# A SwiGLU kernel's first loads: which engine's queue issues the transposing load of tokens 256 to 511, and in which order the first matmul groups run

## The chip, the cores and the metric

The kernel runs on one core of one Trainium2 chip. The metric is the device time of one execution in microseconds (us). A separate profiled execution gives the page and the trace; its times count from the start of its span.

## What is computed

```
x: (1, 2048, 512), w_gate, w_up: (512, 1376), w_down: (1376, 512), all bf16
g = silu(x @ w_gate)
u = x @ w_up
out = (g * u) @ w_down
```

## The kernel before

TensorE contracts over 128 partitions, so x is needed transposed: `xT_sb` holds x as [128 of D, 4 slices of D, 2048 tokens]. The hidden size 1376 is cut into ten full slices of 128 and a rest of 96. The tokens are worked in four chunks `c` of 512 (`SC`). For each chunk and each full slice `ft` there is a gate group (kind G) and an up group (kind U): four matmuls over D each into one PSUM bank. ScalarE takes silu of the gate's bank into `sg_sb` (L280), VectorE multiplies it with the up bank into `hT_sb` (L289). The rest of 96 is done in groups X (L370) and Y (L381). After all chunks the groups O multiply by w_down (L394, L408, L431), VectorE and ScalarE copy the banks to `o_sb`, and SyncE stores them.

All engines run their instructions in program order, with semaphores between them. The part that the change touches is the start, which works on tokens 0 to 511:

- The first half of chunk 0, tokens 0 to 255 (`HT` = 256), comes by a plain load `xn` (256 KB) and is transposed on TensorE against an identity matrix (groups T, L346). VectorE and ScalarE copy the four results to `xT_sb` (L293, L280), ScalarE those of the upper half of D.
- The second half, tokens 256 to 511, comes by a transposing DMA, `x0b` (`load_x`, L87). So do the later chunks, `x1` to `x3`.
- The gate and up weights come in slabs of slices: `wg0`/`wu0` (slice 0, 128 KB each), `wg1`/`wu1` (slice 1, 128 KB each), `wg2`/`wu2` (two slices), `wg4`/`wu4` (three) and `wg7`/`wu7` (the rest), by `load_w` (L92). `wut` is the last 32 columns of w_up.
- `loads_on_scalar` issues `wg0` and `wu0` from ScalarE's queue; `loads_on_sync` issues all others from SyncE's queue in the order written there. After its issues ScalarE runs a dummy activation (L269), ahead of which stands the load of its function table.
- TensorE starts with eight matmuls on constants (L337: six of 512 columns, two of 128). It then waits for `xn` and runs the transposes.
- Then come the groups of slices 0 and 1, named `g0`, `u0`, `g1`, `u1` in the code. They are run in pieces, since tokens 0 to 255 are there earlier than 256 to 511: `g0` and `u0` on tokens 0 to 127 and 128 to 255 (eight matmuls of 128 columns each), `g1` and `u1` on tokens 0 to 255 (four of 256 columns each), and then all four on tokens 256 to 511 (four of 256 columns each). `gu_matmuls` waits (`need`) for the loads that a piece reads. From slice 2 on a group is four matmuls of 512 columns.

The order of the pieces before:

```
for g in (g0, u0):
    gu_matmuls(g, 0, P)
    gu_matmuls(g, P, HT)
gu_matmuls(g1, 0, HT)
gu_matmuls(u1, 0, HT)
for g in (g0, u0, g1, u1):
    gu_matmuls(g, HT, SC)
```

Of the kernel before, what the change touches and what calls it, by code (L numbers as in the profile page):

```python
# [13 lines left out]
def bass_standalone__swiglu_ffn__prompt_kernel(nc, x, w_gate, w_up, w_down, out):  # L14
# [7 lines left out]
    SC = 512  # L22
# [6 lines left out]
    HT = SC // 2  # L29
# [15 lines left out]
    with ExitStack() as es:  # L45
# [29 lines left out]
        loads = {}  # L75

        def load_sem(name):
            loads[name] = sem(f"s_{name}")
            return loads[name]
# [6 lines left out]
        def load_x(eng, name, t0, t1):  # L86
            eng.dma_start_transpose(  # L87
                xT_sb[:, :, t0:t1], xf[t0:t1, :]
            ).then_inc(load_sem(name), 16)

        def load_w(eng, name, src, base, f0, f1):
            eng.dma_start(  # L92
                w_sb[:, :, base + f0:base + f1],
                src[:, f0:f1].rearrange("(k p) f -> p k f", p=P),
            ).then_inc(load_sem(name), 16)

        slabs = [(0, 1), (1, 2), (2, 4), (4, 7), (7, NFT)]
        slab_of = {ft: a for a, b in slabs for ft in range(a, b)}

        def load_slab(eng, a, b):  # L100
            load_w(eng, f"wg{a}", w_gate, 0, a * P, min(b * P, F))
            load_w(eng, f"wu{a}", w_up, UPH, a * P, min(b * P, F - 32))

        def loads_on_scalar(act):
            load_slab(act, *slabs[0])

        def loads_on_sync(sp):
            sp.dma_start(
                xn_sb[:, :, :].rearrange("p j d -> p (j d)"), xf[0:HT, :].rearrange("(p j) d -> p (j d)", j=NXN)
            ).then_inc(load_sem("xn"), 16)  # L110
            load_slab(sp, *slabs[1])
            load_x(sp, "x0b", HT, SC)
            for a, b in slabs[2:]:
                load_slab(sp, a, b)
            load_w(sp, "wut", w_up, F - (F - 32), F - 32, F)
            for c in range(1, NSC):
                load_x(sp, f"x{c}", c * SC, (c + 1) * SC)
            sp.dma_start(
                wd_sb[:, 0:NFF, :], w_down[0:NFF * P, :].rearrange("(k p) d -> p k d", p=P)
            ).then_inc(load_sem("wd"), 16)  # L120
            for c in range(NSC):
                sp.dma_start(
                    wdt_sb[R * c:R * (c + 1), :, :], w_down[NFF * P:F, :].rearrange("(q p) d -> p q d", p=R)
                ).then_inc(load_sem(f"wdt{c}"), 16)
            sp.dma_start(wdl_sb[:, :], w_down[NFF * P:F, LASTA:D]).then_inc(load_sem("wdl"), 16)
# [7 lines left out]
        def add_group(kind, **what):  # L133
            g = dict(kind=kind, at=len(groups), bank=banks[len(groups) % NB], readers=[], **what)
            groups.append(g)
            return g
# [71 lines left out]
        for i in range(NXN):  # L208
            for h, eng in enumerate("DA"):
                g = add_group("T", i=i, h=h)  # L210
                op = add_op(
                    eng, g, kind="copy", out=xT_sb[:, 2 * h:2 * h + 2, i * P:(i + 1) * P],
# [15 lines left out]
        for at in range(NST):  # L228
# [5 lines left out]
            for c0, c1 in halves:  # L234
                g = add_group("O", t=t, c0=c0, c1=c1, c=c)
                if c0 == 0:
                    quads[j].append(g)
                else:
# [3 lines left out]
                    eng, g, kind="copy", out=o_sb[ob][:, c0:c1], src=g["bank"][:, 0:c1 - c0],  # L242
# [6 lines left out]
        def rows_of(t):  # L249
            if t < NXN:  # L250
                return of[0:HT, :].rearrange("(p j) d -> j p d", j=NXN)[t]
            return of[t * P:(t + 1) * P, :]

        def on_sync(sp):
            loads_on_sync(sp)
            for t, c0, c1, ob, eng, n in stores:
                sp.wait_ge(s_A if eng == "A" else s_D, n)
                sp.dma_start(rows_of(t)[:, c0:c1], o_sb[ob][:, c0:c1]).then_inc(s_out[ob], 16)
            for i in range(NOS):
                sp.wait_ge(s_out[i], 16 * n_store[i])  # L260

        def on_gpsimd(pool):
            pool.iota(
                diag[:, :], pattern=[[-1, P]], base=0, channel_multiplier=1,
            ).then_inc(s_I, 1)

        def on_scalar(act):
            loads_on_scalar(act)
            act.activation(adummy[:, 0:4], zero_c, ACT.Silu)  # L269
            for op in act_ops:  # L270
                act.wait_ge(s_P, op["g"]["at"] + 1)
                if op["kind"] == "silu":
                    if op["free"]:
                        act.wait_ge(s_D, op["free"])
                    fn = ACT.Silu
                else:
                    if op["stored"][1]:
                        act.wait_ge(*op["stored"])
                    fn = ACT.Copy
                act.activation(op["out"], op["src"], fn).then_inc(s_A, 1)  # L280
# [15 lines left out]
        def on_tensor(pe):  # L296
            landed = set()

            def need(name):
                if name not in landed:  # L300
                    pe.wait_ge(loads[name], 16)
                    landed.add(name)
# [3 lines left out]
            def after(eng, n):  # L306
                if n > read[eng]:
                    pe.wait_ge(s_A if eng == "A" else s_D, n)
                    read[eng] = n
# [6 lines left out]
            def gu_matmuls(g, n0, n1):  # L316
                c, ft = g["c"], g["ft"]
                if c > 0:
                    need(f"x{c}")
                if c == 0 and n1 > HT:  # L320
                    need("x0b")
                need(("wg" if g["kind"] == "G" else "wu") + str(slab_of[ft]))
                col = (0 if g["kind"] == "G" else UPH) + ft * P
                for dk in range(KD):
                    if c == 0 and dk % 2 == 0:
                        for i in range(n0 // P, min(n1 // P, NXN)):
                            after(*xt_ready[i, dk // 2])
                    ins = pe.matmul(  # L328
                        g["bank"][:, n0:n1], lhsT=w_sb[:, dk, col:col + P],
                        rhs=xT_sb[:, dk, c * SC + n0:c * SC + n1], start=(dk == 0), stop=(dk == KD - 1),  # L330
                    )
                if n1 == SC:
                    ins.then_inc(s_P, 1)
# [15 lines left out]
            g0, u0, g1, u1 = groups[NT:NT + 4]  # L349
            for g in (g0, u0):  # L350
                gu_matmuls(g, 0, P)
                gu_matmuls(g, P, HT)
            gu_matmuls(g1, 0, HT)
            gu_matmuls(u1, 0, HT)
            for g in (g0, u0, g1, u1):
                gu_matmuls(g, HT, SC)

            for g in groups[NT + 4:]:
                kind = g["kind"]
# [73 lines left out]
                skip_group_check=True,  # L433
            ).then_inc(s_P, 1)

        on_sync(nc.sync)
        on_gpsimd(nc.gpsimd)
        on_scalar(nc.scalar)
        on_tensor(nc.tensor)
        on_vector(nc.vector)  # L440

# [27 lines left out]
```

## Time and profile before

| | |
|---|---|
| median of 3 runs | 120.57 us (120.52 to 120.98) |
| the profiled execution's own time | 120.32 us |
| its span | 118.9 us |
| granted TensorE clock, mean over the span | 1.00 |
| TensorE (PE) busy | 115.4 us, 97% |
| VectorE (DVE) busy | 47.3 us, 40% |
| ScalarE (ACT) busy | 31.0 us, 26% |
| DMA queue q1 (SyncE's) | 8.48 MB, 26.7% of 16 engines' span |
| DMA queue q10 (ScalarE's) | 0.26 MB, 1.0% of 16 engines' span |

The span goes from the first to the last of the program's own instructions; the time of the execution has some more around it. PEld is TensorE's weight load, which runs beside its matmuls. A name with a q behind it (SPq, ACTq) is an engine's sequencer, which issues DMAs. In the views a duration of one instruction is in ns and all else in us. "Idle before" is what an engine waited ahead of a group of instructions, and the name behind the arrow is what ended most of that wait. The time "to landing" of a DMA runs from the start of its issue to the semaphore that tells of its last byte. In the timeline the first two columns are start and duration. Some records of matmuls are missing from the trace.

### The profile page before, as it was taken

To read this page: it belongs to the slowest core of one execution; us is meant where nothing else is said; L and a number is where in the kernel's file an instruction comes from. 1 tells how busy PE (TensorE), PEld (TensorE's weight loads), DVE (VectorE), ACT (ScalarE), POOL (GpSimd) and SP (SyncE) were. 2 spreads that over 40 slices of the span, in tenths; PEclk is the share of its full clock that TensorE was granted. 3 is DMA by queue.
4 is the path that set the end of the run, shared out by engine and by line. 5 is a ranking of instruction groups with operands and counts; after the bars stand their busy time and mean duration, and the time that the engine had idled before them with its cause. 6 is when DMAs were issued, how large, how long until landed. Compare 5 with 4: busy or idle time off the path is not lost.

```text
span 118.9 us, 1519 instructions
## 1 busy us (share of the span) xinstructions
PE 115.4 (97%) x600; PEld 54.1 (45%) x611; DVE 47.3 (40%) x73; ACT 31.0 (26%) x53; POOL 0.4 (0%) x5
## 2 busy tenths in 40 slices
PE   7999999999999999999999999999999999999993
PEld 2774444444444444444444444344434444444452
DVE  0133443353443444433444334469617422006530
ACT  4344324454234363244262343230000000000001
POOL 1000000000000000000000000000000000000000
PEclk9999999999999999999999999999999999999999
DMA  3999999970000000000000000000004221002412
GB/s 103 271 307 357 264 162 242 328 183 24 0 0 0 6 0 0 0 3 3 0 0 0 6 0 0 0 0 0 0 0 138 88 88 44 0 0 75 145 50 88
DMA packets 17559, 8.84 MB, mean 74 GB/s; under 512 B 10640, under 2 KB 17424, under 8 KB 17552
## 3 DMA queue, kind: packets, MB, share of 16 engines
q1 hardware_dynamic: 16496, 8.48, 26.7%
q10 hardware_dynamic: 1056, 0.26, 1.0%
q8 instruction: 5, 0.08, 0.3%
q14 instruction: 2, 0.02, 0.1%
HBM read 4.81 MB, written 2.10 MB: 58 GB/s over the span
## 4 chain that ended last, share of the span: by engine, by line
PE 97%; issue 1%; DVE 0%
PE bank L328 58%; PE bank L394 29%; PE bank L370 3%; PE bank L337 2%; PE bank L408 2%; PE bank L381 2%; PE bank L346 1%; DVE o_sb L293 0%; PE bank L431 0%
## 5 line engine op out<-in xcount | busy, mean ns | idle before, releaser
L328 PE MATMUL bank<-xT_sb,w_sb 128*128 128x512 bf16 (+2 forms) x338 | 69.7, 364 | 0.4
L328 PEld LDWEIGHTS bank<-xT_sb,w_sb 128*128 128x128 bf16 x344 | 32.8, 98 | 36.4 <-issue 0.2
L289 DVE TENSOR_TENSOR hT_sb<-sg_sb,bank 128x512 bf16<-128x512 f32 x40 | 27.5, 688 | 40.5 <-PE bank L328 36.6
L394 PE MATMUL bank<-wd_sb,hT_sb 128*128 128x512 bf16 (+2 forms) x166 | 34.5, 366 | 0.4 <-issue 0.3
L280 ACT ACTIVATE sg_sb<-bank 128x512 f32<-128x512 f32 x40 | 23.8, 596 | 40.8 <-PE bank L328 40.8
L394 PEld LDWEIGHTS bank<-wd_sb,hT_sb 128*128 128x128 bf16 x170 | 16.1, 98 | 19.1 <-issue 1.3
L293 DVE CAST o_sb<-bank 128x512 bf16<-128x512 f32 (+1 forms) x16 | 10.1, 663 | 22.0 <-PE bank L408 12.3
L280 ACT ACTIVATE o_sb<-bank 128x384 bf16<-128x384 f32 x1 | 0.5, 492 | 37.8 <-PE bank L394 37.8
L289 DVE TENSOR_TENSOR ht_sb<-sgy_sb,bank 32x512 bf16<-32x512 f32 x8 | 5.5, 684 | 0.2
L289 DVE TENSOR_TENSOR ht_sb<-sgx_sb,bank 32x512 bf16<-32x512 f32 x4 | 2.8, 691 | 3.5 <-ACT sgx_sb L280 3.5
L370 PE MATMUL bank<-xT_sb,w_sb 128*128 128x512 bf16 x15 | 4.1, 379 | 0.1
L337 PE MATMUL bank<-const-bfloat16-1.0 128*128 128x512 bf16 (+1 forms) x8 | 2.9, 545 | 0.8 <-PEq L454 0.8
L280 ACT ACTIVATE sgx_sb<-bank 32x512 f32<-32x512 f32 x4 | 2.4, 588 | 4.5 <-PE bank L370 4.5
L408 PE MATMUL bank<-wdt_sb,ht_sb 32*128 32x512 bf16 (+1 forms) x48 | 2.9, 372 | 0.0
L370 PEld LDWEIGHTS bank<-xT_sb,w_sb 128*128 128x128 bf16 x16 | 1.6, 98 | 1.9
L280 ACT ACTIVATE sgy_sb<-bank 64x512 f32<-64x512 f32 x4 | 2.4, 590 | 0.1
L337 PEld LDWEIGHTS bank<-const-bfloat16-1.0 128*128 128x128 bf16 x8 | 1.0, 136 | 2.4 <-issue 2.4
L381 PE MATMUL bank<-xT_sb,w_sb 128*64 128x512 bf16 x16 | 1.9, 382 | 0.0
L408 PEld LDWEIGHTS bank<-wdt_sb,ht_sb 32*128 32x128 bf16 x48 | 1.1, 93 | 1.7 <-issue 0.8
L269 ACT ACT_TABLE_LOAD x1 | 1.3, 1283 | 1.8 <-issue 1.8
L293 DVE COPY xT_sb<-bank 128x256 bf16<-128x256 bf16 x2 | 0.6, 292 | 2.7 <-PE bank L346 2.7
L381 PEld LDWEIGHTS bank<-xT_sb,w_sb 128*64 128x64 bf16 x16 | 0.8, 109 | 1.0 <-DVE hT_sb L289 0.4
(14 smaller groups left out, 4.0 us busy)
## 6 DMA issues: line engine op xcount, KB each, us to landing
out_dram<-o_sb SPq DMA_DIRECT2D x15, 128.0 KB, 1.7
wd_sb<-in_w_down_dram SPq DMA_DIRECT2D x1, 1280.0 KB, 9.2
w_sb<-in_w_gate_dram SPq DMA_DIRECT2D x1, 480.0 KB, 5.9
w_sb<-in_w_up_dram SPq DMA_DIRECT2D x1, 448.0 KB, 6.5
w_sb<-in_w_gate_dram SPq DMA_DIRECT2D x1, 384.0 KB, 4.5
w_sb<-in_w_up_dram SPq DMA_DIRECT2D x1, 384.0 KB, 5.1
wdt_sb<-in_w_down_dram SPq DMA_DIRECT2D x4, 96.0 KB, 7.5
xn_sb<-in_x_dram SPq DMA_DIRECT2D x1, 256.0 KB, 2.8
```

What stands on the lines that cost most here:

```text
L269: act.activation(adummy[:, 0:4], zero_c, ACT.Silu)
L280: act.activation(op["out"], op["src"], fn).then_inc(s_A, 1)
L289: ins = dve.tensor_tensor(op["out"], op["a"], op["b"], ALU.mult)
L293: ins = dve.tensor_copy(op["out"], op["src"])
L328: ins = pe.matmul(g["bank"][:, n0:n1], lhsT=w_sb[:, dk, col:col + P], rhs=xT_sb[:, dk, c * SC + n0:c * SC + n1], start=(dk == 0), stop=(dk ...
L337: pe.matmul(banks[NB - 1][:, 0:width], lhsT=ones_w, rhs=ones_m[:, 0:width], start=True, stop=True)
L346: ins = pe.transpose(tview(g["bank"])[:, k, :], xn_sb[:, g["i"], dk * P:(dk + 1) * P], ident[:, :])
L370: ins = pe.matmul(g["bank"][:, :], lhsT=w_sb[:, dk, XC0:XC0 + P], rhs=xT_sb[:, dk, c * SC:(c + 1) * SC], start=(dk == 0), stop=(dk == KD - 1),
L381: ins = pe.matmul(g["bank"][y0:y1, :], lhsT=w_sb[:, dk, YC0:YC0 + 64], rhs=xT_sb[:, dk, c * SC:(c + 1) * SC], start=(dk == 0), stop=(dk == ...
L394: ins = pe.matmul(g["bank"][:, 0:c1 - c0], lhsT=hT_sb[:, fk, t * P:(t + 1) * P], rhs=wd_sb[:, fk, c0:c1], start=(start and fk == 0), stop= ...
L408: ins = pe.matmul(g["bank"][:, 0:c1 - c0], lhsT=ht_sb[R * c:R * (c + 1), q, j * P:(j + 1) * P], rhs=wdt_sb[R * c:R * (c + 1), q, c0:c1], s ...
```

## The change

ScalarE issues one DMA ahead of its table load instead of two: the transposing load `x0b`. SyncE issues `xn` and then all slabs in order, `wg0` and `wu0` among them, and `x0b` no longer. Ahead of the next transposing load, `x1`, SyncE waits for the landing of `x0b`. On TensorE the pieces of `g0`, `u0` and `g1` on tokens 256 to 511 run ahead of the two pieces of `u1`. The engines' programs are also written down in another order (ScalarE's first), so that the semaphore of `x0b` exists when SyncE's program names it; each engine's own order isn't touched by that.

```diff
         def loads_on_scalar(act):
-            load_slab(act, *slabs[0])
+            load_x(act, "x0b", HT, SC)
 
         def loads_on_sync(sp):
             sp.dma_start(
                 xn_sb[:, :, :].rearrange("p j d -> p (j d)"), xf[0:HT, :].rearrange("(p j) d -> p (j d)", j=NXN)
             ).then_inc(load_sem("xn"), 16)
+            load_slab(sp, *slabs[0])
             load_slab(sp, *slabs[1])
-            load_x(sp, "x0b", HT, SC)
             for a, b in slabs[2:]:
                 load_slab(sp, a, b)
             load_w(sp, "wut", w_up, F - (F - 32), F - 32, F)
+            sp.wait_ge(loads["x0b"], 16)
             for c in range(1, NSC):
                 load_x(sp, f"x{c}", c * SC, (c + 1) * SC)
...
             gu_matmuls(g1, 0, HT)
+            for g in (g0, u0, g1):
+                gu_matmuls(g, HT, SC)
             gu_matmuls(u1, 0, HT)
-            for g in (g0, u0, g1, u1):
-                gu_matmuls(g, HT, SC)
+            gu_matmuls(u1, HT, SC)
...
+        on_scalar(nc.scalar)
         on_sync(nc.sync)
         on_gpsimd(nc.gpsimd)
-        on_scalar(nc.scalar)
         on_tensor(nc.tensor)
         on_vector(nc.vector)
```

## The prediction

> **What bounds the kernel now.** I read the page's busy times and chain first, then the chain in order of time, then the timeline of the first 9 us by engine, the tile view of the activations, and last the DMA view of the first 4 us.
>
> ```profile
> PE 115.4 (97%) x600; PEld 54.1 (45%) x611; DVE 47.3 (40%) x73; ACT 31.0 (26%) x53; POOL 0.4 (0%) x5
> ```
>
> TensorE is busy 115.4 of 118.9 us, so nothing that only moves other engines can gain. The chain in order of time shows what is left of its idleness at the front:
>
> ```profile
> 0.77 2.93 PE bank L337 x8
> 3.71 0.70 PE bank L346 x8
> 4.41 0.07 issue
> 4.47 3.87 PE bank L328 x40
> 8.35 0.05 issue
> 8.40 10.74 PE bank L328 x49
> ```
>
> Warm-up, eight transposes, then matmuls without a break. The pieces "issue 0.05" come about every 49 matmuls; 600 matmul records stand against 611 weight loads, so a piece of that kind is a lost record, not a stall. The change touches only what lies before 8.4 us. Who waits there:
>
> ```profile
> PEld bank L328 <- issue: 0.2, 1, 0.2
> PEld bank L328 <- DMA xT_sb<-in_x_dram: 0.2, 1, 0.2
> PEld bank L346 <- issue: 0.2, 1, 0.2
> ```
>
> The middle line is the one wait for the load that the change hurries, x0b. In the single records x0b lands at 6.38, the next weight load starts at 6.42 and its matmul at 6.42 instead of 6.37: the matmuls lost 0.05 us. That is all an earlier x0b can win. The wait at L346 is for xn: it lands at 3.49, the transposes start at 3.63, the first copies at 4.04 and 4.22, the first matmul at 4.47. Any delay of xn goes through this path.
>
> The timeline of ScalarE and SyncE, then the four transposing loads in the tile view (duration min/median/max in ns):
>
> ```profile
> 0.73 0.46 ACTq L92 DMA_DIRECT2D w_sb<-in_w_gate_dram  x1
> 1.22 0.53 ACTq L92 DMA_DIRECT2D w_sb<-in_w_up_dram  x1
> 1.78 1.28 ACT L269 ACT_TABLE_LOAD   x1 [1.78 <-issue]
> 4.22 0.66 ACT L280 ACTIVATE xT_sb<-bank 128x256 bf16<-128x256 bf16 x2 [0.94 <-PE bank L346]
> ...
> L87 SPq DMA_TRANSPOSE xT_sb<-in_x_dram x4: 1690/2386/4537, 2.2 to 16.5; - x4
> ```
>
> ScalarE's order is issue, table load, dummy, transpose copies, and it has 0.94 us to spare before the copies. The DMA view of 0 to 4 us, one slice per 0.1 us:
>
> ```profile
> GB/s 0 0 0 0 0 0 0 0 0 0 0 0 0 0 0 0 0 41 225 246 328 287 328 307 351 136 126 220 225 287 266 233 189 210 243 279 279 292 287 287
> ...
> xn_sb<-in_x_dram SPq DMA_DIRECT2D x1, 256.0 KB, 2.8
> w_sb<-in_w_gate_dram ACTq DMA_DIRECT2D x1, 128.0 KB, 3.2
> w_sb<-in_w_gate_dram SPq DMA_DIRECT2D x1, 128.0 KB, 3.4
> w_sb<-in_w_up_dram ACTq DMA_DIRECT2D x1, 128.0 KB, 3.7
> w_sb<-in_w_up_dram SPq DMA_DIRECT2D x1, 128.0 KB, 3.7
> xT_sb<-in_x_dram SPq DMA_TRANSPOSE x1, 4.2
> ```
>
> Two facts. First, the engines move data from 1.7 us on and are full, some 285 GB/s with 256-byte packets, from 3.5 us, so the order of bytes decides. Second, xn ran alone at about 300 GB/s until 2.45; then ScalarE's first packets came, the total fell to 126, and xn's last 25 of 128 packets (51 KB) took 0.55 us, 93 GB/s by the packet records, while ScalarE's queue moved 50 KB. Whatever shares xn's time slows xn.
>
> **The change part by part.** *Issues.* ScalarE loses two issues (0.46 + 0.53) and gains one DMA_TRANSPOSE. The trace has none on ScalarE and none on an empty queue. Bounds: a plain issue, 0.46, and the longest of the four, 4.54. I take 1.7, the row with the same 256 tokens; 1.8 was measured for one with twice the tokens, and the longer ones end just as earlier loads on SyncE's queue drain. Then 0.73 + 1.7 = 2.43, table load 1.28, dummy 0.20: ScalarE is ready at 3.95, before 4.22: cost nothing, with 0.27 us of cover. Beyond an issue of 1.97 each further us is paid in full.
>
> *Weights.* SyncE's second and third loads now are wg0 and wu0, of the size and shape of wg1 and wu1, which stood there. ScalarE's queue carried 1,024 packets of 256 bytes (page: 1,056 with completions, 0.26 MB) and carries 1,024 such packets again, those of x0b. So the nearest rows for wg0 and wu0 are the landings of wg1 and wu1: 1.20 + 3.4 = 4.58 and 1.66 + 3.7 = 5.33. wg1 and wu1 follow at 128 KB each by 282 GB/s, 0.46 us: 5.79 and 6.25. The lower bound, had the DMA been full since 1.7 us, is some 0.35 us earlier for each, and then none is late.
>
> *Order on TensorE.* No matmul is added. Twelve 256-column matmuls (12 x 0.109 = 1.31 us) move ahead of u1, so wu1's due time goes from 5.94 to 7.25 and x0b's from 6.37 to 5.94. x0b's place on ScalarE's queue is that of wg0 and wu0, landed by 4.87; with the transpose's slower issue I take 5 to 5.5. Both are covered.
>
> *SyncE's wait.* Behind it are x1 to x3 and all of w_down. SyncE gets there at about 8 us (ten weight issues of 0.41 to 0.58 and one of 1.44 from 1.2 on), after x0b's landing even in the before trace (6.38): no stall. Were it 3 us, x1, landed 16.97 and first used at about 23.0, would still be in time. Cost 0, cover 6 us.
>
> *The sum, weights alone.* wg0 at 4.58 plus the 0.07 from landing to matmul: g0 starts 4.65 instead of 4.47; eight matmuls of 0.056 end at 5.10; wu0 lets u0 start at 5.37, end 5.82; wg1 lets g1 start at 5.84 instead of 5.50, end 6.28; 1.31 us of second halves end at 7.59; u1, eight times 0.109, at 8.46. Before it was 8.18. So **+0.28 us**; by the lower bound of the landings -0.05 us.
>
> *The sum, xn.* What share xn loses depends on when x0b's first packet comes, which no row shows. Earliest: 0.73 + 0.87 (the stores' issue to first packet) = 1.60; latest: 2.45, when wg0's came. By the count of packets x2's first came 1.35 us after its issue, behind those of x1, so I take 2.05. Of xn 94 packets, 192 KB, are then left: 51 KB in the first 0.55 us, as in the row, and 141 KB at half of 285 GB/s, 0.99 us; xn ends at 3.59 instead of 3.02, +0.57. The latest start gives 0; the earliest, before any of xn, +0.8 (256 KB from 1.7: 0.55 + 205 / 142 = 2.0, an end at 3.7 to 3.8). A late xn also lets the transposes run after 4.02, where the spacing of the 128-column matmuls falls from 0.107 to 0.056, which gives back 0.1; x0b's 0.05 is gained. So xn alone gives +0.42 (bounds -0.05 and +0.65), and it hides the late wg0, wu0 and wg1 (first due at 4.47 + 0.47, landed 4.58). The two sums are not added: they are the same bytes met at different gates. I take **+0.4 us**.
>
> [...]
>
> The profiled execution took 120.32, its span 118.9 plus 1.4 around it: 120.72 after. It lies 0.25 below the median of the three runs, 120.57, so on their scale I forecast 121.0.
>
> **The rivals.**
>
> *ScalarE comes late (slower).* If its transposing issue takes as long as the third such row, 2.98, it ends at 3.71, the table load and dummy at 5.2, and the copies start 1.0 us after 4.22. The first accumulation needs ScalarE's half, so the loss is about +1.0 less 0.05: 121.5. It decides from an issue of 1.97 us. For: only 0.27 us of cover, and ScalarE's plain issues are some 10% slower than SyncE's (0.46 to 0.41). Against: the long rows had a loaded queue ahead; this one is first. 12%.
>
> *xn held behind all of x0b (slower).* ScalarE's issue starts 8 ns before SyncE's. If the 1,024 packets go first, xn's data waits 1.0 us (x0b's own packets took 4.8 to 5.75), xn lands at 4.4 and the loss is some +0.85: 121.4. For: nothing but the order of issue. Against: wg0 was issued 8 ns earlier too and came 0.7 us after xn. 11%.
>
> *TensorE's clock rises late (slower).* The warm-up matmuls are spaced 0.427 us at 512 columns, later ones 0.216; the step is at 4.02. The warm-up ends at 3.5, exactly when xn lands. [...] The granted clock in the profile's rows is 1.00 throughout and does not show the step, so no row prices a hole. 5%. [...]
>
> *x0b's packets come late (slightly faster).* If they start after 3.0, xn is alone to its end, lands near 3.1, the transposes follow the warm-up at 3.53, wg0 and wu0 land in time and x0b still lands before 5.94: -0.15, so 120.4. For: a transposing issue may hand out packets slowly. Against: x2's 1.35 us. 12%.
>
> **How the numbers follow.** 0.5% of 120.57 is 0.6 us, about what a measurement of this kernel can tell from no change. The likeliest case (60%) is 121.0, its own range 120.5 to 121.3, its upper end past 0.6. No path gives a gain of 0.6, since the idle time that can be removed is 0.05 to 0.2: faster 0.02. Slower by 0.6 or more: 12 + 11 + 5, and some 6 from the likeliest case: 0.34. Same: 0.64. The range runs from the fast rival, 120.4, to 121.8, above the first two slow rivals' prices; it leaves out the clock's rival and the tails.
>
> **What would show it.** In the changed profile: xn's landing (3.49 before) moves to 3.7 to 4.2; TensorE's first L328 matmul to 4.65 to 5.0; wg0 and wu0 land near 4.6 and 5.3; the wait for x0b is gone; the stretch from 8.5 us on has the old length. ScalarE's DMA_TRANSPOSE below 1.97 us and its copies released by TensorE, not by the table load, would rule out the first rival. The forecast is wrong if the first 512-column matmul (8.18 before) starts later than 8.8 or earlier than 8.0, or if a wait appears after it.

## The result, and the profile after

| | before | after |
|---|---|---|
| median of 13 runs each | 120.76 us (120.31 to 121.31) | 121.12 us (120.88 to 123.2) |
| ratio after / before | | 1.0041, 95% interval 1.0025 to 1.0057 |
| the profiled execution, its span | 120.32, 118.9 us | 121.26, 119.9 us |

Ratios leave out executions more than 1.5% above the fastest of their kernel (of the changed kernel the one at 123.2). By the ratio the change costs 0.3 to 0.7 us, 0.5 in the middle: slower, with the middle (0.41%) below the 0.5% that the chances were drawn by and the upper end (0.57%) above it. The forecast was +0.4 us.

The two profiled executions differ by 1.0 us of span, twice as much; below it turns out that about half of this is not the change's. First the chain in order of time, of after (start, duration, what):

```profile
0.74 0.40 SPq L108
1.14 0.06 issue
1.20 3.80 DMA w_sb<-in_w_gate_dram
5.00 0.05 issue
5.04 18.13 PE bank L329 x104
```

Before, it started with TensorE's own warm-up and transposes. Now it starts with SyncE's issues and runs through the load of wg0, issued at 1.20 and landed at 5.00. From 5.04 on it is TensorE up to the last copy and store. The waits of after, ahead of the first weight matmul:

```profile
PEld bank L329 <- DMA w_sb<-in_w_gate_dram: 0.7, 1, 0.7
PE bank L329 <- DMA w_sb<-in_w_gate_dram: 0.5, 1, 0.5
```

Only wg0 is waited for. ScalarE's timeline of after:

```profile
0.74 1.32 ACTq L87 DMA_TRANSPOSE xT_sb<-in_x_dram  x1
2.09 1.28 ACT L270 ACT_TABLE_LOAD   x1 [2.09 <-issue]
3.39 0.21 ACT L270 ACTIVATE act_dummy<-const-float32-0.0 128x4 f32<-128x4 f32 x1
4.19 0.81 ACT L281 ACTIVATE xT_sb<-bank 128x256 bf16<-128x256 bf16 x2 [0.60 <-PE bank L347]
```

The transposing issue takes 1.32 us, ScalarE is ready at 3.59, and its copies are released by TensorE (L347), not by itself. In the DMA view of the first 5 us, of after:

```profile
xn_sb<-in_x_dram SPq DMA_DIRECT2D x1, 256.0 KB, 2.7
w_sb<-in_w_gate_dram SPq DMA_DIRECT2D x2, 128.0 KB, 3.8
...
xT_sb<-in_x_dram ACTq DMA_TRANSPOSE x1, 4.5
```

xn was not held up: 2.7 us to landing (2.8 before), at 3.43. The weight loads are: 3.8 us to landing instead of 3.4 in the same place. The landings of the single records and the start of the stream, in us, for both kernels, each also from a second profile that was taken later (runs 10 and 11 below). In the first profile of before the record of the first 512-column matmul is missing; 8.18 is the start of the next one, 8.40, less their spacing of 0.22:

| | xn | wg0 | wu0 | wg1 | wu1 | x0b | first weight matmul | first 512-column matmul | span |
|---|---|---|---|---|---|---|---|---|---|
| before | 3.49 | 3.93 | 4.87 | 4.58 | 5.33 | 6.38 | 4.47 | 8.18 | 118.9 |
| before, again | 3.55 | 3.96 | 4.91 | 4.55 | 5.39 | 6.41 | 4.53 | 8.36 | 119.1 |
| after | 3.43 | 5.00 | 5.55 | 5.99 | 6.45 | 5.25 | 5.04 | 9.20 | 119.9 |
| after, again | 3.58 | 5.06 | 5.62 | 6.08 | 6.67 | 5.34 | 5.11 | 8.76 | 119.5 |

x0b lands 1.1 us earlier, wg0 1.1 us later, and the first weight matmul starts 0.57 later. From the first 512-column matmul to the end of the span all four profiles take 110.7 us, and so do the nine other profiles below (110.72 to 110.75, by the same reckoning where that record is missing): whatever any of these kernels lose in their profiles, they lose ahead of that matmul.

### The profile page after: what moved, and what is told of

It is laid out like the page before. It is cut to its first block, busy times and chain, and to the rows that moved or that the text cites. A ratio compares the mean times of both kernels' runs of the same rounds, so it can differ in the third digit from the quotient of the medians.

```text
span 119.9 us, 1530 instructions
## 1 busy us (share of the span) xinstructions
PE 116.8 (97%) x611; PEld 55.0 (46%) x611; DVE 47.3 (39%) x73; ACT 31.1 (26%) x53; POOL 0.4 (0%) x5
## 4 chain that ended last, share of the span: by engine, by line
PE 94%; DMA 3%; SPq 0%; DVE 0%; issue 0%
PE bank L329 58%; PE bank L396 29%; DMA w_sb<-in_w_gate_dram 3%; PE bank L372 3%; PE bank L410 2%; PE bank L383 2%; SPq L108 0%; DVE o_sb L294 0%; PE bank L433 0%
## 5 line engine op out<-in xcount | busy, mean ns | idle before, releaser
L329 PEld LDWEIGHTS bank<-xT_sb,w_sb 128*128 128x128 bf16 x344 | 33.5, 100 | 36.6 <-DMA w_sb<-in_w_gate_dram 0.7
L396 PE MATMUL bank<-wd_sb,hT_sb 128*128 128x512 bf16 (+2 forms) x170 | 35.1, 367 | 0.0
L372 PEld LDWEIGHTS bank<-xT_sb,w_sb 128*128 128x128 bf16 x16 | 1.6, 98 | 1.9
```

The source lines that it names most:

```text
L329: ins = pe.matmul(g["bank"][:, n0:n1], lhsT=w_sb[:, dk, col:col + P], rhs=xT_sb[:, dk, c * SC + n0:c * SC + n1], start=(dk == 0), stop=(dk ...
L372: ins = pe.matmul(g["bank"][:, :], lhsT=w_sb[:, dk, XC0:XC0 + P], rhs=xT_sb[:, dk, c * SC:(c + 1) * SC], start=(dk == 0), stop=(dk == KD - 1),
L396: ins = pe.matmul(g["bank"][:, 0:c1 - c0], lhsT=hT_sb[:, fk, t * P:(t + 1) * P], rhs=wd_sb[:, fk, c0:c1], start=(start and fk == 0), stop= ...
```

## The experiments

The theory after this look: what counts is wg0's landing, late because x0b's 1,024 packets share the DMA engines with it. Rivals: the new order of pieces and the place on SyncE's queue. A third one, contention later on, is already out by the equal 110.7 us. In the edits only the changed lines stand. Experiments 1, 4, 6 and 7 edit the changed kernel, the others the one before. [+x, +y] is the 95% interval of the difference to before, from the ratio times 120.6 us.

**1. The changed loads, the old order of pieces**

```diff
-            for g in (g0, u0, g1):
-                gu_matmuls(g, HT, SC)
             gu_matmuls(u1, 0, HT)
-            gu_matmuls(u1, HT, SC)
+            for g in (g0, u0, g1, u1):
+                gu_matmuls(g, HT, SC)
```

> The changed loads with the old order of pieces on TensorE (u1's first half ahead of all second halves). Theory: the loss is wg0's late landing (5.00 instead of 3.93 us) beside x0b's packets on ScalarE's queue, so this is as slow as the changed kernel, +0.35 to +0.5 us against before, first matmul at 5.0 to 5.1. Rival, the new order of pieces costs the time: then this returns to 0 against before. By wu1's landing (6.45) and the old order's due time for it (6.48 in the changed kernel) the order should change less than 0.1 us.

Ratio 1.0055 (1.0033 to 1.0077): [+0.40, +0.93] us, from 9 of its 12 executions: as slow as the changed kernel, or slower. The three others took 123.02 to 123.30; what they may be is said under the clock's rival below. In its profile wg0 landed at 5.14, the first weight matmul started at 5.19, and u0 waited too:

```profile
PEld bank L329 <- DMA w_sb<-in_w_gate_dram: 0.7, 1, 0.7
PEld bank L329 <- DMA w_sb<-in_w_up_dram: 0.4, 1, 0.4
```

The loads carry the loss; the order does not.

**2. The old loads, the new order of pieces** (the same edit the other way round, on the kernel before)

> The old loads with the new order of pieces. Theory: only x0b's due time moves 0.44 us earlier while it still lands at 6.38, so at full clock u1 ends 0.44 later (8.61 instead of 8.17 us); where TensorE is still at half clock there, it arrives later than 6.38 anyway and nothing is lost: between 0 and +0.44, about +0.15 on average. Rival, the new order by itself is the change's loss: +0.4 to +0.5.

Ratio 1.0004 (0.9984 to 1.0024): [-0.19, +0.29]. The rival falls. In its profile the second halves did wait for x0b, landed at 6.32: two matmuls that elsewhere start 0.11 apart start at 5.93 and 6.37, and the span is 119.3; over the runs that is lost in the scatter.

**3. Plain packets in x0b's place**

```diff
         def loads_on_scalar(act):
-            load_slab(act, *slabs[0])
+            load_slab(act, *slabs[1])
...
-            load_slab(sp, *slabs[1])
+            load_slab(sp, *slabs[0])
             load_x(sp, "x0b", HT, SC)
```

> The old kernel with slabs 0 and 1 exchanged between the queues: ScalarE issues wg1 and wu1, SyncE xn, wg0, wu0, x0b. ScalarE's queue has again 1,024 packets of 256 bytes, but plain ones. Theory A, any continuous 256 KB beside it makes wg0 late: wg0 lands at 4.9 to 5.0, first matmul at 5.0, +0.3 to +0.4 us. Theory B, the transposing load is special (one unbroken stream, and SyncE's next packets start later): wg0 lands at 4.58 as wg1 did in its place, first matmul at 4.65, +0.1 to +0.2 us.

Ratio 1.0002 (0.9980 to 1.0024): [-0.24, +0.29]. wg0 landed at 4.71 and the first weight matmul came at 4.76. The chain of this kernel:

```profile
1.20 3.51 DMA w_sb<-in_w_gate_dram
4.71 0.04 issue
4.76 4.54 PE bank L328 x40
```

wg0's landing is nearer to theory B. The packet records, counted in the order of time, say where the two part. wg0's 512 packets ran from 3.37 to 4.29 here and from 3.35 to 4.25 in the changed kernel: 128 KB in 0.9 us, some 145 GB/s, half of 285 beside either neighbour. But from the last packet to the landing it took 0.42 us here and 0.75 in the changed kernel (0.69 in its second profile, 0.71 in experiment 1, 0.67 in experiment 4, always with x0b's packets beside wg0's). The 4-byte packets behind wg0's tell the same: they end at 4.38 here, 0.33 ahead of the landing, and at 4.42 in the changed kernel, 0.58 ahead of it.

**4. ScalarE's table load first**

```diff
+            act.activation(adummy[:, 0:4], zero_c, ACT.Silu)
             loads_on_scalar(act)
-            act.activation(adummy[:, 0:4], zero_c, ACT.Silu)
```

> The changed kernel with ScalarE's table load and dummy activation ahead of its transposing issue, which so starts at about 2.3 us instead of 0.74; SyncE's queue is untouched. Theory: x0b's packets start at about 4.1 instead of 2.65, wg0 lands at 3.9 to 4.1 and the first matmul is back at 4.4 to 4.5; x0b lands at 6.0 to 6.4 and takes some of it back; 0 to +0.2 us. Rival, the place as second on SyncE's queue alone makes wg0 late: wg0 still lands near 5.0, +0.35 to +0.5 us or more.

Ratio 1.0030 (1.0011 to 1.0049): [+0.13, +0.59]. It did not do what it was made for: ScalarE's sequencer issued x0b at 0.80 us beside the running table load (0.74 to 2.03), so x0b came no later, wg0 landed at 5.07 and the time is that of the changed kernel. With the table load back at the front the loss is still there, so it is not that load's new place that costs.

**5. A longer warm-up** (before, with `N_FILL = 7` instead of 2)

> The old kernel with seven instead of two 128-column warm-up matmuls: TensorE's transposes start 5 x 0.107 = 0.53 us later, as long as the changed kernel's wait for wg0, and no DMA is touched. Theory: a pure delay of TensorE's start by 0.53 us, less the 0.05 of the wait for x0b, less what the later start saves of work at half clock: first matmul at 4.9 to 5.0, +0.25 to +0.4 us, about what the change costs. Rival, the change's cost is in contention later on and not in the late start: then a late start alone hides and this is within 0.1 us of before.

Ratio 0.9996 (0.9976 to 1.0017): [-0.29, +0.21]. A miss: the transposes started at 4.03 instead of 3.63 and the first weight matmul at 4.92 instead of 4.47, and no loss is seen over the runs. The profile offers a reason:

```profile
L328 PE MATMUL bank<-xT_sb,w_sb 128*128 128x128 bf16 x16 | 1.7, 294 | 0.0
L346 PE MATMUL bank<-ident,xn_sb 128*128 128x128 bf16 x8 | 1.1, 311 | 0.0
```

The mean of the 128-column weight matmuls is 294 ns; in the first profile of before it is 220. TensorE ran at half speed (107 ns between 128-column matmuls, and 56 after the step) up to 6.39 us here and up to 4.02 there, so by this account only a part of a delay there is lost: what is put off is done later at double speed. The same group in after:

```profile
L329 PE MATMUL bank<-xT_sb,w_sb 128*128 128x128 bf16 x16 | 1.7, 290 | 0.5 <-DMA w_sb<-in_w_gate_dram 0.5
```

and in after again:

```profile
L329 PE MATMUL bank<-xT_sb,w_sb 128*128 128x128 bf16 x16 | 1.2, 221 | 0.4 <-DMA w_sb<-in_w_gate_dram 0.4
```

The same kernel, the same wait, and 0.4 us between the spans (119.9 and 119.5).

**6. wg0 back in front on ScalarE, x0b behind it**

```diff
         def loads_on_scalar(act):
+            load_w(act, "wg0", w_gate, 0, 0, P)
             load_x(act, "x0b", HT, SC)
...
-            load_slab(sp, *slabs[0])
+            load_w(sp, "wu0", w_up, UPH, 0, P)
```

> The changed kernel with wg0 back as ScalarE's first DMA and x0b behind it on the same queue; SyncE issues xn, wu0, wg1, wu1 and so on. Theory: wg0 lands at 3.9 to 4.0 again and the first matmul is at 4.4 to 4.5; wu0, second on SyncE's queue, lands at 4.6 to 4.8, x0b by 5.9: the changed kernel's loss is gone, -0.1 to +0.1 us against before. Rival, the transposing load slows SyncE's queue wherever it stands on ScalarE's: wu0 at 5.2 or later, u0 waits, +0.2 to +0.4 us.

Ratio 1.0027 (1.0006 to 1.0048): [+0.07, +0.58]. The first half of the expectation held: wg0 at 3.98, first weight matmul at 4.52, wu0 at 4.58. The second missed: wg1 landed at 5.99 instead of 4.58, and x0b at 6.23 instead of by 5.9. By the packet records SyncE's queue stood idle from 4.09 to 4.46 while x0b's packets flowed (3.63 to 5.21), though wg1 had been issued at 1.66. The loss moved from wg0 to wg1, due at 5.50 at the full clock.

**7. x0b's issue held to 2.26 us**

```diff
+        s_T = sem("s_T")
...
-            loads_on_scalar(act)
-            act.activation(adummy[:, 0:4], zero_c, ACT.Silu)
+            act.activation(adummy[:, 0:4], zero_c, ACT.Silu).then_inc(s_T, 1)
+            act.wait_ge(s_T, 1)
+            loads_on_scalar(act)
```

> The changed kernel with ScalarE's transposing issue held back, by a semaphore, until its dummy activation is done, so at about 2.3 us; SyncE's queue is untouched. Theory: x0b's packets start at about 4.2, wg0 lands at 3.9 to 4.1 and the first matmul is at 4.4 to 4.5; wg1 and x0b are later in exchange, some waits of 0.1 to 0.4 us further on: 0 to +0.3 us. Rival, the second place on SyncE's queue makes wg0 late whatever runs beside it: wg0 near 5.0, first matmul at 5.0, +0.4 us or more.

Ratio 1.0162 (1.0113 to 1.0210): [+1.36, +2.53], from four of its six executions; the six took 122.18 to 124.49. For wg0 the theory held, and the rival fell: second on SyncE's queue, with nothing from ScalarE's beside it, it landed at 3.97 and the first weight matmul started at 4.51. But the price was far above the expected 0.3 us: wu0 landed at 6.15, wg1 at 7.10, x0b at 8.20, and TensorE waited for each:

```profile
PE bank L331 <- DMA w_sb<-in_w_up_dram: 0.8, 1, 0.8
PE bank L331 <- DMA xT_sb<-in_x_dram: 0.5, 1, 0.5
PE bank L331 <- DMA w_sb<-in_w_gate_dram: 0.3, 1, 0.3
```

This run also shows what the neighbour does to wg0. Its packets ran from 2.72 to 3.48 here, beginning before xn's had ended (3.09), and the landing trailed them by 0.49. In the changed kernel they began at 3.35, 0.38 after xn's last packet, while x0b's flowed: 0.63 us later. They then took 0.14 longer, and the landing trailed by 0.26 more. The late beginning is the largest part of the 1.03 us, and beside the plain packets of experiment 3 it was as late (3.37).

**8. All loads on SyncE's queue** (before, without `loads_on_scalar(act)`, `load_slab(sp, *slabs[0])` behind xn)

> The old order of pieces and the old place of x0b, with all loads on SyncE's queue: xn, wg0, wu0, wg1, wu1, x0b and the rest; ScalarE issues none. Theory: alone on the DMA engines, xn lands at 3.2 to 3.4, wg0 at 3.9 to 4.1, wu0 near 4.5, wg1 near 4.9, x0b at 6.4 as before: within 0.15 us of before. Rival, the second place on SyncE's queue is what makes wg0 late: wg0 at 4.6 to 5.0, first matmul at 4.7 to 5.1, +0.2 to +0.5 us.

Ratio 1.0036 (1.0016 to 1.0056): [+0.19, +0.68]. Again wg0 is early in the second place (3.90, first weight matmul 4.46), and again something else is late: wu0 at 5.47 and x0b at 7.51, with no load on the other queue. The DMA view of this kernel from 2 to 6 us, 0.1 us a slice:

```profile
GB/s 61 246 287 389 410 430 348 305 315 295 287 269 146 133 120 97 51 51 51 97 169 192 205 205 243 261 269 243 256 205 277 282 284 289 289 274 256 215 159 97
```

From 3.2 us on, when wu0's packets are due, the rate falls, to 51 GB/s from 3.6 to 3.9.

**9. A bare wait on TensorE** (before, with `need("wu1")` ahead of the first weight matmul)

> The old kernel with one wait added on TensorE: its first weight matmul waits for wu1 (landed at 5.33) and not for wg0 only, so it starts at 5.35 to 5.45 instead of 4.47; no DMA and no order is touched. Theory: an idle wait at this place is paid by the rest of the stream: +0.72 us (0.91 less the waits of 0.19 that it covers) where the full clock is there by 5 us, +0.4 to +0.5 where it comes later, since the work that is put off then runs at the full clock; about +0.55 on average. Rival, after the longer warm-up cost nothing: a late start hides altogether, within 0.2 us of before.

Ratio 1.0021 (1.0004 to 1.0039): [+0.05, +0.47], from the 8 of 13 executions that the ratio keeps (120.95 to 121.25). So an idle wait at this place does cost time with every DMA as before, though in these eight at the most 0.47 where 0.55 was expected; a late start doesn't hide altogether. The five others took 122.81 to 123.20; with them the means differ by 1.05 us (121.82 against 120.76). The profiled execution was one of the five, with a span of 121.8. Its first weight matmuls, and the window from 7 to 9.7 us:

```profile
L328 PE MATMUL bank<-xT_sb,w_sb 128*128 128x128 bf16 x16 | 1.9, 313 | 0.7 <-DMA w_sb<-in_w_up_dram 0.7
...
L328 PE MATMUL bank<-xT_sb,w_sb 128*128 128x256 bf16 x13 | 2.9, 418 | 0.0
```

418 ns instead of 273, and 13 of them took 2.9 us, 0.22 each, where the kernel before started one every 0.11: half speed, up to 9.83 us.

**10 and 11. Both kernels once more, unchanged**

> The old kernel, unchanged, for another profile. Theory: the step of TensorE's spacing from 107 to 56 ns (128 columns) is the execution's own and comes anywhere between 4.0 and 6.5 us, with the landings as in the first profile (xn 3.5, wg0 3.9, x0b 6.4); a step after 6 us gives a span of 119.6 to 119.9 instead of 118.9. Rival, the step is the kernel's: 4.0 us again and a span of 118.9.

> The changed kernel, unchanged, for another profile. Theory: wg0 lands near 5.0 and the first matmul starts at 5.0 to 5.2 again; with a step of the clock before 5 us the span is 119.3 to 119.5, with one after 6 us 119.9 as in the first profile. Rival, the late step belongs to the changed kernel: it comes at 6.4 us again.

The rows are in the table above. The spacing steps from 107 to 56 ns at 5.2 us in before again (4.02 in the first profile) and before 5.1 in after again (6.4 in the first). Both rivals fall: the step is the execution's own. A span of 119.6 to 119.9 for a late step in the kernel before was not seen, as its step came at 5.2. The spans, 119.1 and 119.5, differ by 0.4 us, and so do the first 512-column matmuls (8.36 and 8.76).

## Why the prediction came out right, and where its steps failed

The number held: +0.4 forecast, +0.5 (0.3 to 0.7) measured. Of its two sums the wrong one was made the likeliest, so the closeness of the number is luck: +0.42 was the price of a late xn, which did not come, and the sum with the right mechanism gave +0.28.

- *xn as the gate: failed.* The step "I take 2.05" for x0b's first packet, with bounds of 1.60 to 2.45, was off: it came at 2.67 (2.84 in the second profile), outside both. xn's packets ended at 2.97, and xn landed at 3.43 instead of 3.7 to 4.2. Its term was +0.42 and is about -0.05.
- *The weights: right mechanism, too small.* The step that took the landings of wg1 and wu1 for those of wg0 and wu0 gave 4.58, 5.33, 5.79, 6.25; measured 5.00, 5.55, 5.99, 6.45. Of the 0.42 us at wg0, 0.13 is the packets' end (4.25, wg1's was 4.12) and 0.29 the longer way from last packet to landing (0.75, wg1's was 0.46). By experiment 3 that longer way goes with the transposing neighbour; why it does isn't shown. The same sum with the measured landings: 5.04 + 0.45 = 5.49; u0 from 5.59 to 6.04; g1 to 6.48; 1.31 more; u1 ends at 8.66. That is +0.48 instead of +0.28.
- *Order, SyncE's wait, ScalarE: right.* Experiment 2 bounds the order at 0.29 us, no stall shows on SyncE (x1 issued at 8.29, 8.86 before), and the first rival is out by its own condition, an issue of 1.32 against 1.97 us. "xn held behind all of x0b" and "x0b's packets come late" are out by xn's landing; x0b's first packet did come late, but not after 3.0.
- *What would show it.* The first weight matmul was to be at 4.65 to 5.0 and is at 5.04, and the first 512-column matmul was to start by 8.8: 9.20 in the first profile, 8.76 in the second. By that mark the first profile said wrong. What the prediction took for fixed is the clock: "the step is at 4.02" was one execution's.
- *The clock as a rival, 5%.* No run shows whether, or how far, a hole behind the warm-up puts TensorE's step off, so this share of the chance of slower rests on no row. What the runs showed in its place: in experiment 9, with 0.7 us of idleness, one step at 9.83 us is on record, in an execution whose span of 121.8 is some 2 us above those of the eight kept ones (119.6 to 119.8). In the changed kernel's own two profiles, with holes of 0.5 and 0.4 us, the step came at 6.4 and before 5.1, so it is not what moved its median. The run at 123.2 and experiment 1's three at 123.02 to 123.30 left no profile, so whether they were of this kind isn't shown. But they lie where experiment 9's five lie, while none of the 94 executions of the kernel before (the 13 above and those run beside the experiments) took more than 121.31. With that one run the changed kernel's mean is 0.57 us above the mean before (121.33 and 120.76): the rival is no explanation of the median, and likely a part of the price.

The account of the loss rests on three shown things: second on SyncE's queue, wg0 lands at 3.9 to 4.0 with nothing on ScalarE's, at 4.7 beside plain packets and at 5.0 to 5.1 beside x0b (experiments 7, 8 and 3, and the four profiles with the changed loads), a bare wait at this place costs time (9), and the loads without the order cost as much as both (1). How much of the wait an execution pays depends, by this account, on its clock: +0.48 by the sum at full speed, less where the work that was put off would have run at half. The 0.4 between the second profiles fits. Why experiment 5's late start shows no loss at all over its runs stays open, and experiment 3's, 0.29 us late, shows none either; the half speed accounts for a part. No version tried beats the kernel before.

## What to carry to other kernels

When a load is moved to another queue, read the landings of the loads beside it, and not its own alone. Here wg0, second on SyncE's queue, landed at 3.90 and 3.97 with nothing on ScalarE's (experiments 8 and 7), at 4.71 beside plain packets (3) and at 5.00 beside x0b: a load that was not needed yet and went out first on an idle queue made the one that all waited for begin later (3.35 instead of 2.72), run longer (0.90 us instead of 0.76) and land late. Moving it back was not enough by itself: in experiments 6, 7 and 8 wg0 was early again, another load was late in its stead, and time was lost all the same. When the spans of two profiled executions differ by more than their medians, look for a part that differs between executions of one kernel (here the spacing of TensorE's first matmuls) before pricing the change by them.

## What the runs showed of the hardware that was not expected

- TensorE's step to full speed (128-column matmuls 56 ns apart instead of 107) came anywhere from 3.4 to 6.5 us in twelve of these profiles (between 3.40 and 3.74 in experiment 4, at 4.02 and 5.2 before, before 5.1 and at 6.4 after) and at 9.83 in experiment 9's, while the granted clock in the rows is 1.00 throughout. What sets its time, and why the step at 9.83 came so late, isn't shown.
- One queue alone can run far below its later rate: 51 GB/s in the slices of experiment 8 where two queues together moved some 285 (before, at the same time), and 38 GB/s at 3.9 us in experiment 7, before x0b's first packet. Later the same single queue moves 284 to 289 GB/s. Its cause was not tried and stays open.
- The first packet of x0b came 1.9 to 2.2 us after the start of its issue where it was the first load on ScalarE's queue, that of xn, a plain load of 128 packets, 1.0 to 1.4 us after.
- wg0's landing trailed its last packet by 0.67 to 0.75 us in the four profiles in which x0b's packets flowed beside it and by 0.33 to 0.49 in the nine others. This is no rule for every load: wu0's landing trailed by 1.33 in experiment 1, and by 1.04 in experiment 8 (by the same count of packets), where ScalarE's queue had no load at all.
